# Moving the softmax scale into the copies of q and k, and the row maximum into a plain reduce

## The chip, the cores and the metric

The kernel runs on one core of one Trainium2 chip. Its time is what the device takes for one execution, in microseconds (us). Three runs of the kernel before gave 871.57, 875.91 and 878.39 us, so its median is 875.91 us. One more execution was profiled; it took 872.72 us, and the rows of the profile belong to that one. The engines are called PE (TensorE; its weight loads have a row of their own, PEld), DVE (VectorE), ACT (ScalarE), POOL (GpSimd) and SP (SyncE, which here only issues DMAs).

## The reference

Attention that looks only inside a cluster, and then a feed-forward network with a maximum of three products (B = 4, H = 8, S = 768, D = 64, 16 clusters; 3072 tokens of 512, hidden width 768):

```python
scale = 1.0 / np.sqrt(D)
mask = q_assign[:, :, :, None] == k_assign[:, :, None, :]
scores = scale * np.matmul(q, k.transpose(0, 1, 3, 2))
scores = np.where(mask, scores, -1000000000.0)
scores = scores - np.max(scores, axis=-1, keepdims=True)
attn = np.exp(scores)
attn = attn / (np.sum(attn, axis=-1, keepdims=True) + 1e-09)
out = np.matmul(attn, v)
...
h = np.maximum(np.maximum(x @ w1, x @ w2), x @ w3)
return (h @ w_out).astype(np.float32)
```

`q_assign` and `k_assign` are the cluster whose normalised centroid has the largest product with the row. Since D is 64, the scale is 0.125.

## The kernel before

**Steps.** The attention is cut into 192 steps: 4 batches, 8 heads, 6 blocks of 128 query rows. One step is one call of `scores` (L472): it fills a score tile of 128 x 768 fp32 in PSUM, takes the maximum of each row, the exponential, and the factor 1/sum, splits the result into two fp16 parts and hands them to a DMA that transposes them. Three steps make a group, and `av` (L501) multiplies a group's transposed weights by v. When both heads of a pair are done, `x_split` (L518) makes the input of the FFN.

**Operands.** For a pair of heads the tile `qk` has four planes, AQ, BQ, BK and AK, of 128 rows. A load brings q (64 rows, D of them) and k (64 more) of one head as `stage`; L362 rounds it to fp32r into BQ, and L365 puts the rest that the rounding left into AQ. `qk_moves` (L367) then arranges them: two ACT copies put k's high part into the upper halves of AK (L371) and BK (L372), a DMA brings k's low part to the lower half of AK (L373), and POOL copies q's high part to the lower half of AQ (L374). For the first pair `first_k_moves` (L377) and `first_q_moves` (L385) do this without the DMA, with L381 to L383 on ACT and L388 on POOL. The lower rows of BQ and BK get 16 rows of cluster marks, so that the matrix product itself subtracts a huge number where the clusters differ.

**One step.** Four matmuls (L477, L479) fill the score tile; `big` has three such PSUM buffers, shared with the cluster scores (L405, L406, L413). Then L482 on DVE reads the tile, writes it back multiplied by -1/sqrt(D), and gives through its accumulator the minimum of each row, `nm`, which is the negated maximum of the scaled scores. In the profile it is a pair, TENSOR_SCALAR_CACHE_REDUCE and DVE_READ_ACCUMULATOR. L485 on ACT takes exp(-1 * tile + nm) into SBUF with the row sums `r`; with it the PSUM buffer is free. L486 and L487 on DVE make the factor of each row. In 147 steps ACT applies it and rounds to fp16 (L495) and DVE makes the low part (L496); in 45 steps (`by_pool`) POOL does the multiplication and the low part (L491, L493) and ACT the rounding (L492). L497 on SP issues the transposing DMA from `hl` (four buffers) to `pt` (two).

**Order.** Beside the steps run the preparation of the weights, of v and of the next pair, and the FFN of the group or batch before (`hidden`, L548 to L567, and `outp`, L582 to L593). A table of due steps (`plan`) and priorities (`at_prio`) say when each may come; the last batch's FFN comes after all steps. The order on each engine's queue is then made by the program's scheduler out of these priorities and of modelled durations (`schedule_with_timeline_sim=True`, L761). Each queue runs in its order.

Of the kernel before, what the change touches and what calls it, by code (L numbers as in the profile page):

```python
# [8 lines left out]
F32 = mybir.dt.float32  # L9
# [5 lines left out]
AF = mybir.ActivationFunctionType  # L15
ALU = mybir.AluOpType
AX = mybir.AxisListType
# [6 lines left out]
def kernel(  # L24
# [23 lines left out]
    nc = tc.nc  # L48
    B, H, D, S = qk.shape
    D = D // 2  # L50
# [20 lines left out]
    def big():  # L71
        return ps_big.tile([P, 2 * 512], F32, tag="big", name="big")
# [46 lines left out]
    last = {}  # L119
# [223 lines left out]


    AQ, BQ, BK, AK = range(4)
    HALF = ((0, 512), (512, S))
    qkt = {}
    masks = {}

    def load(b, h):  # L350
        x = stage()
        nc.sync.dma_start(out=x, in_=qk[b, h])
        return x
# [3 lines left out]
    def qk_prep(b, pr, i, pool, again=False):  # L357
# [6 lines left out]
        eng = nc.vector if (b, pr) < (1, 1) and QK_LO[b * NPAIR + pr + (b == 0 and again) * (NPAIR + 1)] else nc.gpsimd  # L364
        last["lo"] = eng.tensor_tensor(t[:, AQ, i], x, t[:, BQ, i].bitcast(F32), op=ALU.subtract)  # L365

    def qk_moves(b, pr):  # L367
        t = qkt[b, pr]
        x = t.bitcast(F32)
        up, dn = slice(0, D), slice(D, 2 * D)  # L370
        nc.scalar.copy(t[up, AK], x[dn, BQ])  # L371
        nc.scalar.copy(t[up, BK], x[dn, BQ])  # L372
        nc.sync.dma_start(out=t[dn, AK].bitcast(F32), in_=x[dn, AQ])  # L373
        nc.gpsimd.tensor_scalar(t[dn, AQ], x[up, BQ], 1.0, 1.0, op0=ALU.mult, op1=ALU.mult)  # L374


    def first_k_moves(xs):  # L377
        t = qkt[0, 0]
        up, dn = slice(0, D), slice(D, 2 * D)
        for i in range(2):  # L380
            nc.scalar.copy(t[up, BK, i], xs[i][dn])  # L381
            nc.scalar.copy(t[up, AK, i], xs[i][dn])
            nc.scalar.copy(t[dn, AK, i], t[dn, AQ, i].bitcast(F32))  # L383

    def first_q_moves():  # L385
        t = qkt[0, 0]
        for i in range(2):
            nc.gpsimd.tensor_scalar(t[D : 2 * D, AQ, i], t[0:D, BQ, i].bitcast(F32), 1.0, 1.0, op0=ALU.mult, op1=ALU.mult)  # L388

    def qk_masks(b, pr):  # L390
        t = qkt[b, pr].bitcast(F32)
# [7 lines left out]
    def cluster_scores(b, pr):  # L399
        t = cl[b, pr] = big()  # L400
        x = qkt[b, pr]
        for lo, hi in HALF:
            for i in range(2):
# [4 lines left out]
    def cluster_early(b, pr):  # L408
        t = cl[b, pr] = big()
        xs = [load(b, 2 * pr + i) for i in range(2)]  # L410
        for lo, hi in HALF:
            for i in range(2):
# [44 lines left out]
    def prep_units(b, pr, pool, again=False):  # L457
        u = [lambda i=i: qk_prep(b, pr, i, pool, again) for i in range(2)]
        if again:
            f = [qk_moves, qk_masks, v_prep]  # L460
        else:
            f = [cluster_scores, qk_moves, cluster_rows] + [v_prep] * (b > 0)
        u += [lambda g=g: g(b, pr) for g in f]
        return u


    K2 = D + C
    SCALE = 1.0 / D**0.5

    def scores(b, h, qt, pt, g, by_pool):  # L472
        aq, bq, bk, ak = (qkt[b, h // 2][:, j, h & 1] for j in range(4))
        t = big()
        qs = slice(qt * P, (qt + 1) * P)
        for lo, hi in HALF:
            nc.tensor.matmul(t[:, lo:hi], aq[:, qs], ak[:, lo:hi], start=True, stop=False)  # L477
        for lo, hi in HALF:
            last["pe"] = nc.tensor.matmul(t[:, lo:hi], bq[0:K2, qs], bk[0:K2, lo:hi], start=False, stop=True)  # L479
        nm = sb.tile([P, 1], F32, tag="nm", name="nm", bufs=6)  # L480
        e = t[:, 0:S]
        last["nm"] = nc.vector.tensor_scalar(e, e, -SCALE, 3.0e38, op0=ALU.mult, op1=ALU.min, accum_out=nm)  # L482
        r = sb.tile([P, 1], F32, tag="r", name="r", bufs=6)
        x = sb.tile([P, S], F32, tag="e", name="e", bufs=3)
        nc.scalar.activation(x, e, AF.Exp, bias=nm, scale=-1.0, accum_out=r)  # L485
        nc.vector.tensor_scalar(r, r, 1.0e-9, 2.0**-14, op0=ALU.add, op1=ALU.mult)  # L486
        nc.vector.reciprocal(r, r)  # L487
        pace[:] = [r[0:1]]
        hl = sb.tile([P, 2, S], F16, tag="hl", name="hl", bufs=4)
        if by_pool:  # L490
            nc.gpsimd.tensor_scalar(x, x, r, 1.0, op0=ALU.mult, op1=ALU.mult)  # L491
            nc.scalar.copy(hl[:, 0, :], x)  # L492
            nc.gpsimd.tensor_tensor(hl[:, 1, :], x, hl[:, 0, :], op=ALU.subtract)  # L493
        else:
            nc.scalar.activation(hl[:, 0, :], x, AF.Copy, scale=r)  # L495
            nc.vector.scalar_tensor_tensor(hl[:, 1, :], x, r, hl[:, 0, :], op0=ALU.mult, op1=ALU.subtract)  # L496
        last["dma"] = nc.sync.dma_start_transpose(out=pt[:, g], in_=hl.rearrange("p a s -> p (a s)"))  # L497
# [159 lines left out]
    with tc.issue_after(last["cw_hi"].ins), tc.issue_after(last["cw_lo"].ins):  # L657
        first[1]()
    cluster_scores(0, 0)
    behind("hi", first_k_moves, xin)  # L660
    first_q_moves()
    behind("lo", vm[0])
    cluster_rows(0, 0)
# [28 lines left out]
    for b in range(B):  # L692
# [3 lines left out]
        if b:  # L696
            visits += [(b, pr, tuple(range(NG))) for pr in range(NPAIR)]
            for pr in range(NPAIR):
                if (b, pr) > (1, 0):
                    t = at + pr * 2 * V  # L700
# [10 lines left out]
    for b, pr, gis in visits:  # L711
        for gi in gis:
            x = (
                sb.tile([P, NB], F32, tag="xs", name="xs", bufs=1),
                sb.tile([P, NB], F32, tag="xt", name="xt", bufs=1),
            )
            for h in (2 * pr, 2 * pr + 1):
                pt = sb.tile([P, G, 2 * QT, P], F16, tag="pt", name="pt", bufs=2)
                for g in range(G):
                    at_prio(step, scores, b, h, gi * G + g, pt, g, by_pool(step))  # L720
                    run_step()
                    step += 1
                units = [lambda a=(b, h, gi, pt, *x): behind("pe", av, *a)]
                if h & 1:
                    units.append(lambda a=(b, pr, gi, *x): x_split(*a))
                plan.setdefault(step + AV_LAG - 1, []).extend((step + AV_LATE, u) for u in units)
# [38 lines left out]
```

## Time and profile before

| what | value |
|---|---|
| median of three runs | 875.91 us |
| the profiled execution | 872.72 us |
| its span from the first to the last instruction | 870.7 us |
| mean granted PE clock, share of full speed | 0.918 |
| L485, the exponential, on ACT | 192 of 898 ns |
| L496, the low part, on DVE | 147 of 1297 ns |
| transposing DMAs (L497) | 192, landing 4.2 us after the issue |
| bytes moved by DMA | 130.99 MB |

A row of the profile names the line, the engine, the operation, the tiles written and read, the shapes and the count; then the busy time in us and the mean length of one instruction in ns; then for how long the engine stood idle ahead of these instructions, and whom it waited for. A row of a stretch gives, for each engine, its busy time and in brackets how many instructions began there. A row in order of time gives start and duration in us.

### The profile page before, as it was taken

The page shows a single profiled execution, that of the slowest core. Times are in us where ns is not written, and L with a number is a line of the kernel's source. Part 1 is how long each engine was busy: PE and PEld are TensorE (multiplying, and loading weights), DVE is VectorE, ACT ScalarE, POOL GpSimd, SP SyncE. Part 2 cuts the span into 40 slices and gives each one's busy share as a digit, 9 for nine tenths or more (in the row PEclk, how much of TensorE's full clock was granted, in tenths as well). Part 3 has the DMA queues.
Part 4 walks back from the last instruction along what each step waited for, and adds up shares of the span by engine and source line. Part 5 has one row for each costly group of instructions (what it writes and reads, how often), then busy time and mean ns, then how long its engine had stood idle before and what let it go on. Part 6 is the DMA issues. An engine that isn't in the chain of part 4 may idle for free. (4 is left out here: it accounts for less than half of the span.)

```text
span 870.7 us, 12115 instructions
## 1 busy us (share of the span) xinstructions
PE 719.7 (83%) x3836; PEld 421.6 (48%) x3836; DVE 613.3 (70%) x1327; ACT 562.4 (65%) x939; POOL 522.9 (60%) x502
## 2 busy tenths in 40 slices
PE   3533766867868989897898999899998999999997
PEld 2312334434544546454555565555554555556463
DVE  7968888799999759885978776876777666411020
ACT  7655677967967577969595967784968467520101
POOL 4696785677963657685867465685684536412111
PEclk9756586869988999998999999999999999999999
DMA  7873988989978499889797978695778586810000
GB/s 248 220 176 72 198 147 195 235 218 244 194 155 191 123 170 182 176 153 216 136 201 129 204 154 154 125 214 117 148 137 137 118 141 114 152 48 1 37 1 36
DMA packets 327679, 130.99 MB, mean 150 GB/s; under 512 B 304192, under 2 KB 313408, under 8 KB 327616
## 3 DMA queue, kind: packets, MB, share of 16 engines
q1 hardware_dynamic: 327616, 130.22, 72.7%
q8 instruction: 30, 0.49, 0.2%
q14 instruction: 33, 0.27, 0.1%
HBM read 38.57 MB, written 7.08 MB: 52 GB/s over the span
## 5 line engine op out<-in xcount | busy, mean ns | idle before, releaser
L485 ACT ACTIVATE e<-big,nm 128x768 f32<-128x768 f32 x192 | 172.2, 898 | 93.9 <-DVE big L482 39.1
L548 PE MATMUL one<-x,w16a 128*128 128x384 f16 x1152 | 205.6, 332 | 18.4 <-DVE p_w L106 3.7
L496 DVE SCALAR_TENSOR_TENSOR hl<-e,r,hl 128x768 f16<-128x768 f32 x147 | 189.4, 1297 | 34.7 <-ACT hl L495 32.4
L482 DVE TENSOR_SCALAR_CACHE_REDUCE big<-big 128x768 f32<-128x768 f32 x192 | 182.1, 960 | 20.2 <-PE big L479 19.4
L477 PE MATMUL big<-qk 128*128 128x512 f32 (+1 forms) x384 | 127.8, 417 | 61.6 <-ACT e L485 56.8
L495 ACT ACTIVATE hl<-e,r 128x768 f16<-128x768 f32 x147 | 134.9, 930 | 42.0 <-DMA pt<-hl 25.1
L548 PEld LDWEIGHTS <-w16a 128*128 128x128 f16 x1152 | 110.6, 99 | 101.1 <-issue 34.2
L479 PE MATMUL big<-qk 80*128 80x512 f32 (+1 forms) x384 | 108.6, 366 | 8.6 <-DMA qk<-cl_t 4.5
L477 PEld LDWEIGHTS big<-qk 128*128 128x128 f32 x384 | 68.0, 209 | 98.1 <-ACT e L485 72.7
L548 PE MATMUL one<-x,w16b 128*128 128x384 f16 x576 | 104.6, 338 | 5.0 <-ACT xt L516 4.4
L507 PE MATMUL one<-pt,v 128*128 128x384 f16 x384 | 82.2, 351 | 29.7 <-POOL v L339 8.0
L493 POOL TENSOR_TENSOR hl<-e,hl 128x768 f16<-128x768 f32 x45 | 77.6, 1728 | 22.4 <-ACT hl L492 22.1
L548 PEld LDWEIGHTS <-w16b 128*128 128x128 f16 x576 | 56.6, 101 | 47.9 <-issue 15.8
L365 POOL TENSOR_TENSOR qk<-stage,qk 128x768 fp32r<-128x768 f32 x32 | 63.8, 2010 | 23.8 <-ACT qk L362 23.5
L479 PEld LDWEIGHTS big<-qk 80*128 80x128 f32 x384 | 65.4, 207 | 21.8 <-DMA qk<-cl_t 5.0
L491 POOL TENSOR_SCALAR e<-e,r 128x768 f32<-128x768 f32 x45 | 47.8, 1064 | 37.0 <-DVE r L487 26.5
L507 PEld LDWEIGHTS <-v 128*128 128x128 f16 x384 | 36.7, 104 | 61.6 <-issue 33.2
L520 POOL TENSOR_TENSOR xs<-xs,xt 128x384 f32<-128x384 f32 x32 | 34.1, 1065 | 51.9 <-ACT xt L516 51.9
L560 DVE SCALAR_TENSOR_TENSOR vf_h<-one,vf_h 128x384 f32<-128x384 f32 x48 | 26.4, 550 | 47.9 <-PE one L548 47.6
L560 DVE SCALAR_TENSOR_TENSOR wf_h<-one,wf_h 128x384 f32<-128x384 f32 x48 | 26.5, 552 | 46.8 <-PE one L548 43.2
L486 DVE TENSOR_SCALAR r<-r 128x1 f32<-128x1 f32 x192 | 27.0, 145 | 45.8 <-ACT e L485 44.9
L492 ACT CAST hl<-e 128x768 f16<-128x768 f32 x45 | 37.3, 829 | 29.3 <-DMA pt<-hl 18.1
(133 smaller groups left out, 1108.2 us busy)
## 6 DMA issues: line engine op xcount, KB each, us to landing
stage<-in_qk_dram SPq DMA_DIRECT2D x36, 384.0 KB, 4.2
stage<-in_v_dram SPq DMA_DIRECT2D x25, 384.0 KB, 3.8
wd<-in_moe_w_dram SPq DMA_DIRECT2D x18, 512.0 KB, 5.1
qk<-qk SPq DMA_DIRECT2D x16, 384.0 KB, 4.4
out_dram<-o SPq DMA_DIRECT2D x24, 256.0 KB, 2.1
pt<-hl SPq DMA_TRANSPOSE x192, 4.2
wd<-in_moe_w_out_dram SPq DMA_DIRECT2D x6, 512.0 KB, 4.4
qk<-cl_t SPq DMA_DIRECT2D x56, 48.0 KB, 2.1
```

Of the source, the lines that this page charges most:

```text
L365: last["lo"] = eng.tensor_tensor(t[:, AQ, i], x, t[:, BQ, i].bitcast(F32), op=ALU.subtract)
L477: nc.tensor.matmul(t[:, lo:hi], aq[:, qs], ak[:, lo:hi], start=True, stop=False)
L479: last["pe"] = nc.tensor.matmul(t[:, lo:hi], bq[0:K2, qs], bk[0:K2, lo:hi], start=False, stop=True)
L482: last["nm"] = nc.vector.tensor_scalar(e, e, -SCALE, 3.0e38, op0=ALU.mult, op1=ALU.min, accum_out=nm)
L485: nc.scalar.activation(x, e, AF.Exp, bias=nm, scale=-1.0, accum_out=r)
L491: nc.gpsimd.tensor_scalar(x, x, r, 1.0, op0=ALU.mult, op1=ALU.mult)
L493: nc.gpsimd.tensor_tensor(hl[:, 1, :], x, hl[:, 0, :], op=ALU.subtract)
L495: nc.scalar.activation(hl[:, 0, :], x, AF.Copy, scale=r)
L496: nc.vector.scalar_tensor_tensor(hl[:, 1, :], x, r, hl[:, 0, :], op0=ALU.mult, op1=ALU.subtract)
L507: nc.tensor.matmul(t[:, 0:NB], vt, pt[:, :, kt, :], start=(kt == 0), stop=False)
L548: nc.tensor.matmul(t[:, 0:NB], w16[jt // JA][:, jt % JA, wa, i, ct], x16[b, gi, ct][:, xa, :], start=(n == 0), stop=(n == 3 * CT - 1),)
L560: nc.vector.scalar_tensor_tensor(m, t[:, 0:NB], 2.0**-24, ms[jt], op0=ALU.mult, op1=ALU.max)
```

## The change

The factor 1/sqrt(D) is put into the copies of k's high part (AK and BK, upper half) and of q's high part (AQ, lower half); the parts left unscaled meet a scaled one in each product, so every product carries the factor once. The ACT copies become activations with a constant factor; POOL's keep their operation with another constant. The DMA of k's low part moves the same bytes between the same places, with its two sides written with the same type. The row maximum becomes a `tensor_reduce` with a negated result that writes nothing back to PSUM, and the exponential reads the scores with scale 1.

```diff
+    SCALE = 1.0 / D**0.5
...
-        nc.scalar.copy(t[up, AK], x[dn, BQ])
-        nc.scalar.copy(t[up, BK], x[dn, BQ])
-        nc.sync.dma_start(out=t[dn, AK].bitcast(F32), in_=x[dn, AQ])
-        nc.gpsimd.tensor_scalar(t[dn, AQ], x[up, BQ], 1.0, 1.0, op0=ALU.mult, op1=ALU.mult)
+        nc.scalar.activation(t[up, AK], x[dn, BQ], AF.Copy, scale=SCALE)
+        nc.scalar.activation(t[up, BK], x[dn, BQ], AF.Copy, scale=SCALE)
+        nc.sync.dma_start(out=x[dn, AK], in_=x[dn, AQ])
+        nc.gpsimd.tensor_scalar(t[dn, AQ], x[up, BQ], SCALE, 1.0, op0=ALU.mult, op1=ALU.mult)
...
-            nc.scalar.copy(t[up, BK, i], xs[i][dn])
-            nc.scalar.copy(t[up, AK, i], xs[i][dn])
+            nc.scalar.activation(t[up, BK, i], xs[i][dn], AF.Copy, scale=SCALE)
+            nc.scalar.activation(t[up, AK, i], xs[i][dn], AF.Copy, scale=SCALE)
...
-            nc.gpsimd.tensor_scalar(t[D : 2 * D, AQ, i], t[0:D, BQ, i].bitcast(F32), 1.0, 1.0, op0=ALU.mult, op1=ALU.mult)
+            nc.gpsimd.tensor_scalar(t[D : 2 * D, AQ, i], t[0:D, BQ, i].bitcast(F32), SCALE, 1.0, op0=ALU.mult, op1=ALU.mult)
...
-    SCALE = 1.0 / D**0.5
...
-        last["nm"] = nc.vector.tensor_scalar(e, e, -SCALE, 3.0e38, op0=ALU.mult, op1=ALU.min, accum_out=nm)
+        last["nm"] = nc.vector.tensor_reduce(nm, e, axis=AX.X, op=ALU.max, negate=True)
...
-        nc.scalar.activation(x, e, AF.Exp, bias=nm, scale=-1.0, accum_out=r)
+        nc.scalar.activation(x, e, AF.Exp, bias=nm, scale=1.0, accum_out=r)
```

## The prediction

> **What bounds the kernel now.** First the page's busy times, then the busy time of each engine in four stretches (columns: stretch, its length, then busy us and count for PE, its weight loads, DVE, ACT and POOL, the granted PE clock, DMA share, GB/s):
>
> ```profile
> PE 719.7 (83%) x3836; PEld 421.6 (48%) x3836; DVE 613.3 (70%) x1327; ACT 562.4 (65%) x939; POOL 522.9 (60%) x502
> ```
> ```profile
> 100.00:250.00 150.00, 109.77 (x515) 63.94 (x514) 131.43 (x300) 119.99 (x201) 114.39 (x109) 0.82 0.94 203
> 250.00:500.00 250.00, 219.09 (x1191) 128.76 (x1189) 202.84 (x453) 185.46 (x310) 160.15 (x138) 0.95 0.86 170
> 500.00:750.00 250.00, 232.52 (x1339) 139.39 (x1338) 182.08 (x403) 176.33 (x300) 153.95 (x138) 0.99 0.77 142
> 750.00:870.00 120.00, 114.61 (x654) 62.64 (x653) 17.31 (x31) 18.39 (x33) 23.35 (x32) 1.00 0.15 38
> ```
>
> The average share of 70% for DVE hides three different stages. From 100 to 250 us DVE is busy 131.43 of 150 us (88%) and the DMA engines 94%: this is where DVE could be the bound. From 250 on PE takes over: 88%, then 232.52 of 250 (93%). From 750 on only TensorE works, on the last FFN. Whatever DVE gains, it cannot touch these last 120 us, and between 500 and 750 it can win at most the 17.5 us in which PE is idle.
>
> Next, who waits for whom (total, times, longest), and the chain of waits that ended last, which this trace follows back to 494 us only:
>
> ```profile
> PE big L477 <- ACT e L485: 56.8, 35, 5.0
> DVE r L486 <- ACT e L485: 44.9, 36, 7.4
> ACT e L485 <- DVE big L482: 39.1, 15, 8.4
> ```
> ```profile
> by line: PE one L548 10.1%; DMA pt<-hl 5.8%; PE one L582 5.4%; issue 2.8%; ACT e L485 2.3%; ACT hl L495 2.2%; DVE big L482 1.5%; DVE hl L496 1.1%; POOL hl L493 1.1%; PE one L507 0.8%; POOL e L491 0.6%; ACT qk L362 0.5%; ACT xt L516 0.5%; PE
> ...
> 494.00 0.83 ACT hl L495
> ```
>
> No engine is alone to blame: TensorE waits for the exponential to free a score buffer, the exponential waits for the row maximum in only 15 of 192 cases, and DVE itself waits for ACT. L482, the line that changes, is on the chain for 1.5% of 870.7, or 13.1 us, out of 870.7 - 494 = 377 us followed.
>
> **DVE: the row maximum.** These groups price the old pair and the new instruction:
>
> ```profile
> L482 DVE TENSOR_SCALAR_CACHE_REDUCE big<-big 128x768 f32<-128x768 f32 x192 | 182.1, 960 | 20.2 <-PE big L479 19.4
> L482 DVE DVE_READ_ACCUMULATOR big<-big 128x1 f32 x192 | 26.5, 138 | 0.1
> L422 DVE STREAM_TRANSPOSE cl_t<-big 128x768 f32<-128x768 f32 x16 | 15.6, 975 | 11.3 <-DMA qk<-cl_t 8.0 <-PE big L413 2.5 <-PE big L406 0.8
> L440 DVE STREAM_TRANSPOSE cl_t<-onehot 128x768 f32<-128x768 f32 x16 | 15.6, 974 | 0.3
> L293 DVE TENSOR_REDUCE vmax<-stage 128x1 f32<-128x768 f32 x12 | 11.3, 945 | 6.8 <-DMA stage<-in_v_dram 6.8
> L222 DVE TENSOR_REDUCE wmx<-wf 128x1 f32<-128x1536 f32 x6 | 10.5, 1746 | 0.1
> L106 DVE TENSOR_REDUCE p_w<-one 128x1 f32<-128x128 f32 x6 | 1.7, 282 | 0.0
> ```
>
> The reduce exists at this width, but from SBUF: 945 ns. Its slope is (1746 - 945)/768 = 1.043 ns per element, so its fixed part is 945 - 801 = 144 ns, and 128 elements from SBUF would take 277; L106 reads 128 from PSUM and takes 282. PSUM thus costs 5 ns, and the transposes say the same (975 from PSUM, 974 from SBUF). I take 950 ns, between 945 and 960. Negation is not in the trace; L293 and L222 take absolute values, L106 none, and all lie on one line, so a change of sign should be free too.
>
> [...]
>
> The tempting sum is now 960 + 138 - 950 = 148 ns, times 192 = 28.4 us. It is wrong if the accumulator read runs under the next instruction, so look at a bunch of them in order of time on DVE and on ACT (start, duration):
>
> ```profile
> 508.09 0.55 DVE L429 TENSOR_REDUCE cl_m<-cl_t 128x24 f32<-128x384 f32 x1 [2.83 <-POOL cl_t L428]
> 508.56 0.96 DVE L482 TENSOR_SCALAR_CACHE_REDUCE big<-big 128x768 f32<-128x768 f32 x1
> 509.43 0.14 DVE L482 DVE_READ_ACCUMULATOR big<-big 128x1 f32 x1
> 509.43 1.00 DVE L482 TENSOR_SCALAR_CACHE_REDUCE big<-big 128x768 f32<-128x768 f32 x1
> 510.35 0.14 DVE L482 DVE_READ_ACCUMULATOR big<-big 128x1 f32 x1
> 510.35 1.00 DVE L482 TENSOR_SCALAR_CACHE_REDUCE big<-big 128x768 f32<-128x768 f32 x1
> 511.26 0.14 DVE L482 DVE_READ_ACCUMULATOR big<-big 128x1 f32 x1
> 511.26 0.55 DVE L434 SCALAR_TENSOR_TENSOR cl_t<-cl_t,rank 128x384 f32<-128x384 f32 x1
> ```
> ```profile
> 509.67 0.90 ACT L485 ACTIVATE e<-big,nm 128x768 f32<-128x768 f32 x1 [1.79 <-DVE big L482]
> 510.47 0.19 ACT L485 ACTIVATION_READ_ACCUMULATOR e<-big,nm 128x1 f32 x1
> 510.58 0.90 ACT L485 ACTIVATE e<-big,nm 128x768 f32<-128x768 f32 x1
> ```
>
> The instruction behind a read starts at the same stamp as the read (509.43, 510.35, 511.26). L434 behind one takes 0.55, as L429, of the same width and with no read ahead of it, does. Only a second L482 behind a read grows, from 0.96 to 1.00. So a pair costs DVE 0.87 to 0.92 us from start to start. How a reduce hands on:
>
> ```profile
> 34.05 0.95 DVE L293 TENSOR_REDUCE vmax<-stage 128x1 f32<-128x768 f32 x1 [0.68 <-DMA stage<-in_v_dram]
> 34.92 0.96 DVE L482 TENSOR_SCALAR_CACHE_REDUCE big<-big 128x768 f32<-128x768 f32 x1
> ```
>
> After 0.87 us. The saving in DVE throughput is therefore 0 to 0.05 us a step, not 0.148. And where maxima come in bunches, the exponentials behind them come 0.91 apart by their own length (510.58 - 509.67), which covers even the 0.05.
>
> [...]
>
> What is left is delay. The first pair of a bunch ends at 509.43 + 0.14 = 1.01 us after its start and the exponential starts 0.10 us later; a reduce of 0.95 lets it start 0.06 earlier. The cover for most steps is that ACT is still busy or that DVE is behind (only 15 waits above); it counts where L482 is on the chain: 13.1 us at 0.92 a pair is 14 pairs. The steps done meanwhile:
>
> ```profile
> 100.00:250.00 150.00, 38.45 (x78) 0.82 0.94 203
> ...
> 500.00:750.00 250.00, 67.89 (x138) 0.99 0.77 142
> ...
> sum 870.00, DVE 191.13; mean DVE 38.23
> ```
>
> (L482 alone; each step has two instructions, so 69 steps from 500 to 750.) 14 in 69 is one step in five; of 192 that is 39, times 0.06 to 0.07 us = 2.3 to 2.7, and I take 2.6 us off the path.
>
> **ACT and POOL: the copies.** A copy with a scale is an ACTIVATE instead of a CAST. Not seen at 64x1536, so from the nearest rows:
>
> ```profile
> L495 ACT ACTIVATE hl<-e,r 128x768 f16<-128x768 f32 x147 | 134.9, 930 | 42.0 <-DMA pt<-hl 25.1 <-issue 7.2 <-DVE r L487 6.1
> L492 ACT CAST hl<-e 128x768 f16<-128x768 f32 x45 | 37.3, 829 | 29.3 <-DMA pt<-hl 18.1 <-POOL e L491 10.8
> L371 ACT CAST qk<-qk 64x1536 fp32r<-64x1536 f32 x16 | 23.5, 1472 | 0.4
> L558 ACT ACTIVATE vf_h<-one 128x384 f32<-128x384 f32 x24 | 11.7, 486 | 28.7 <-PE one L548 28.2 <-DVE vf_h L560 0.2
> ```
>
> With its factor in a tile ACTIVATE costs 930 - 829 = 101 ns more; with a constant factor (L558, as the new copies have) it takes 486 for 384 elements, where a CAST, at (1472 - 829)/768 = 0.837 ns per element, would take 829 - 321 = 508: 22 less, though from PSUM. 32 copies in L371 and L372 and four at the start make 36, so -0.8 to +3.6 us of ACT time over the run. I take 0, by the constant factor; where one is on the chain, the start of that head pair's scores is late by as much. POOL's copies keep their instruction with another constant, and the DMA between copies moves the same bytes: 0, with the same waits. The exponential keeps form and operands: 0.
>
> **The sum.** 872.7 (the profiled execution, 870.7 of it span) - 2.6 = 870.1. The median of the runs shown, 875.9, lies 3.2 above it; off that median it is 873.3, and I say 873. A measurement of this kernel can tell about 1%, 8.8 us, from no change, so this counts as the same.
>
> **The rivals.**
> *Every step gains its delay.* If maximum, exponential and split form the loop in all 192 steps, 0.07 x 192 = 13.4 us: 862. For it: DVE at 88% in 100 to 250, and the 39.1 us of waits. Against: PE at 93% later, DMA at 94% at just that time.
> [...]
> *The queues come out in a worse order (slower).* The order on each queue is the scheduler's, which works with modelled durations (line 761 asks for it), and the replaced instruction may have another. Place: 100 to 250 us, 39 steps (x78), DMA at 94%, so late transposes cannot be made up. If one more maximum (0.95 us) stands ahead of the split L496 in one of three steps there, 13 x 0.95 = 12.4 us: 888. It decides from 10 steps on (9.5 us). For: three maxima in a row stood ahead of other work at 508.56. Against: most modelled lengths stay, and an order can also turn out better.
> *The copies cost their upper price:* 873.3 + 3.6 = 877, still the same. The change does then what it says and shows nothing.
>
> **How the numbers follow.** My forecast 0.47 and the dear copies 0.06: within 1%, 0.53. Every delay 0.19 and the whole read 0.08: faster, 0.27. Worse order 0.20: slower. The likeliest case's own range is 867 to 884. The range of 8 in 10 reaches from 857, leaving the whole read out (0.08), to 888, where the slower rival begins to be cut in half (0.10).
>
> **What would show it.** Right: L482 is one TENSOR_REDUCE of 945 to 960 ns, 192 of them, no read behind it; DVE's busy time falls by about 9 us only (the 191 us that the pairs cover become 182), not by 28; waiting exponentials start about 0.10 us after the reduce ends; L371 and L372 stay near 1472; PE's idle time per stretch stays. [...]

## The result, and the profile after

| | before | after |
|---|---|---|
| median of 20 runs each, taken in turns | 873.92 us | 869.93 us |
| lowest and highest | 867.88, 878.39 | 860.08, 876.87 |
| ratio, 95% interval | | 0.993 (0.9903 to 0.9958) |
| the profiled execution, and its span | 872.72, 870.7 | 869.84, 867.8 |

That is a small gain, under the 1% that the prediction took for the bound. The ratio compares only runs within 1.5% of the fastest of each kernel, and since one run of the kernel after was very quick (860.08), seven of its twenty fall out; over all twenty the means are 873.61 and 870.13 us, a ratio of 0.996 or 3.5 us, and twelve more runs below give 3.2 us. I go by 3.5 us.

The order of the instructions on the five queues is, apart from the replaced instruction itself, the same in both traces but for two places. On ACT one cast of weights (L206) that stood ahead of an exponential, at 124 us, now stands behind it; on DVE, at 482 us, two small instructions (L486 and L101) stand each ahead of a reciprocal instead of behind it. Before, on ACT and on DVE:

```profile
123.61 1.14 ACT L206 CAST w16a<-wf 128x512 f16<-128x512 f32 x2
124.78 0.90 ACT L485 ACTIVATE e<-big,nm 128x768 f32<-128x768 f32 x1
```
```profile
482.37 0.16 DVE L487 RECIPROCAL r<-r 128x1 f32<-128x1 f32 x1
482.44 0.14 DVE L486 TENSOR_SCALAR r<-r 128x1 f32<-128x1 f32 x1
482.50 0.15 DVE L487 RECIPROCAL r<-r 128x1 f32<-128x1 f32 x1
482.57 0.14 DVE L101 TENSOR_SCALAR sc_m<-sc_m 128x1 int32<-128x1 int32 x1
```

And after:

```profile
118.59 0.62 ACT L206 CAST w16a<-wf 128x512 f16<-128x512 f32 x1
119.23 0.90 ACT L486 ACTIVATE e<-big,nm 128x768 f32<-128x768 f32 x1
120.03 0.19 ACT L486 ACTIVATION_READ_ACCUMULATOR e<-big,nm 128x1 f32 x1
120.12 0.61 ACT L206 CAST w16a<-wf 128x512 f16<-128x512 f32 x1
```
```profile
480.70 0.14 DVE L487 TENSOR_SCALAR r<-r 128x1 f32<-128x1 f32 x1
480.77 0.15 DVE L488 RECIPROCAL r<-r 128x1 f32<-128x1 f32 x1
480.83 0.13 DVE L101 TENSOR_SCALAR sc_m<-sc_m 128x1 int32<-128x1 int32 x1
480.89 0.21 DVE L488 RECIPROCAL r<-r 128x1 f32<-128x1 f32 x2
```

Otherwise the scheduler gives the plain reduce the same place as the pair.

The page's busy times, and the four stretches (columns as before):

```profile
PE 728.8 (84%) x3836; PEld 425.7 (49%) x3836; DVE 606.0 (70%) x1135; ACT 562.0 (65%) x939; POOL 521.5 (60%) x502
```
```profile
100.00:250.00 150.00, 112.27 (x520) 65.18 (x519) 124.97 (x251) 115.74 (x194) 112.09 (x108) 0.80 0.91 197
250.00:500.00 250.00, 221.55 (x1184) 128.61 (x1183) 200.39 (x382) 185.36 (x308) 157.10 (x136) 0.94 0.85 171
500.00:750.00 250.00, 233.47 (x1351) 140.62 (x1349) 180.41 (x337) 178.23 (x303) 154.58 (x138) 0.99 0.77 144
750.00:870.00 120.00, 112.26 (x641) 61.20 (x639) 16.10 (x28) 15.68 (x28) 23.31 (x32) 0.99 0.12 32
```

DVE's count falls by 192, from 1327 to 1135, its busy time by 7.3 us only. The stretches do not tell where: from 100 to 250 us it is 6.5 us less, but in the first 100 us it is 4.5 us more (84.11 against 79.63, the rows below, before and after), as some steps fall into another stretch (39 maxima from 100 to 250 us before, 37 now). TensorE's stretch from 500 to 750 is as full as it was, 233 of 250.

```profile
0.00:100.00 100.00, 43.66 (x142) 26.85 (x143) 79.63 (x146) 62.23 (x99) 71.05 (x86) 0.73 0.72 180
```
```profile
0.00:100.00 100.00, 49.28 (x147) 30.13 (x148) 84.11 (x141) 67.03 (x108) 74.38 (x89) 0.91 0.77 190
```

The changed instructions:

```profile
L483 DVE TENSOR_REDUCE nm<-big 128x1 f32<-128x768 f32 x192 | 179.1, 946 | 25.5 <-PE big L480 24.7
```
```profile
L373 ACT ACTIVATE qk<-qk 64x1536 fp32r<-64x1536 f32 x16 | 23.7, 1484 | 0.4
L374 ACT ACTIVATE qk<-qk 64x1536 fp32r<-64x1536 f32 x16 | 23.4, 1465 | 0.0
```

The reduce from PSUM takes 946 ns, with the negation; 950 was forecast. The copies take 1484 and 1465 ns, much as the plain ones did (1472). Then the bunch of three maxima at the same place of the run, in order of time on DVE and on ACT:

```profile
507.05 0.56 DVE L431 TENSOR_REDUCE cl_m<-cl_t 128x24 f32<-128x384 f32 x1 [2.82 <-POOL cl_t L430]
507.52 2.68 DVE L483 TENSOR_REDUCE nm<-big 128x1 f32<-128x768 f32 x3
510.11 0.55 DVE L436 SCALAR_TENSOR_TENSOR cl_t<-cl_t,rank 128x384 f32<-128x384 f32 x1
```
```profile
508.56 0.90 ACT L486 ACTIVATE e<-big,nm 128x768 f32<-128x768 f32 x1 [1.44 <-DVE nm L483]
509.36 0.19 ACT L486 ACTIVATION_READ_ACCUMULATOR e<-big,nm 128x1 f32 x1
509.45 0.89 ACT L486 ACTIVATE e<-big,nm 128x768 f32<-128x768 f32 x1
510.24 0.20 ACT L486 ACTIVATION_READ_ACCUMULATOR e<-big,nm 128x1 f32 x1
510.33 0.90 ACT L486 ACTIVATE e<-big,nm 128x768 f32<-128x768 f32 x1
```

From the first maximum to the work behind the third it is now 510.11 - 507.52 = 2.59 us, where it was 511.26 - 508.56 = 2.70. The first exponential starts 508.56 - 507.52 = 1.04 us after the first maximum, before 1.11: the 0.07 of the forecast. And the exponentials now follow each other every 0.89 us where they came every 0.91: in the bunch it was DVE that paced them. The prediction had taken the 0.91 for their own length.

```profile
PE big L478 <- ACT e L486: 52.1, 30, 5.4
DVE r L487 <- ACT e L486: 45.2, 36, 7.4
ACT e L486 <- DVE nm L483: 28.7, 14, 4.1
```

The exponential's waits for the maximum fall from 39.1 to 28.7 us in total. Single profiles are no proof of that: the same kernel has 35.3 us of them in its later profile (the changed kernel again, below), and a kernel with the old pair has 29.6 (reads at all three places, below); and two runs of the same kernel are up to 17 us apart (860.08 and 876.87). So the parts were tried one by one. The waits in these two, in this order:

```profile
ACT e L486 <- DVE nm L483: 35.3, 14, 8.2
```
```profile
ACT e L486 <- DVE big L483: 29.6, 15, 4.1
```

### The profile page after: what moved, and what is told of

Read it like the earlier page. It is cut to its first block, busy times and chain, and to the rows that moved or that the text cites. A ratio compares the mean times of both kernels' runs of the same rounds, so it can differ in the third digit from the quotient of the medians.

```text
span 867.8 us, 11919 instructions
## 1 busy us (share of the span) xinstructions
PE 728.8 (84%) x3836; PEld 425.7 (49%) x3836; DVE 606.0 (70%) x1135; ACT 562.0 (65%) x939; POOL 521.5 (60%) x502
## 5 line engine op out<-in xcount | busy, mean ns | idle before, releaser
L486 ACT ACTIVATE e<-big,nm 128x768 f32<-128x768 f32 x192 | 171.8, 896 | 84.8 <-DVE nm L483 28.7
L549 PE MATMUL one<-x,w16a 128*128 128x384 f16 x1152 | 209.3, 337 | 18.1 <-DVE p_w L106 3.8
L497 DVE SCALAR_TENSOR_TENSOR hl<-e,r,hl 128x768 f16<-128x768 f32 x147 | 185.3, 1269 | 33.7 <-ACT hl L496 31.8
L483 DVE TENSOR_REDUCE nm<-big 128x1 f32<-128x768 f32 x192 | 179.1, 946 | 25.5 <-PE big L480 24.7
L478 PE MATMUL big<-qk 128*128 128x512 f32 (+1 forms) x384 | 128.6, 418 | 56.1 <-ACT e L486 52.1
L480 PE MATMUL big<-qk 80*128 80x512 f32 (+1 forms) x384 | 110.9, 373 | 10.8 <-DMA qk<-cl_t 6.8
L508 PE MATMUL one<-pt,v 128*128 128x384 f16 x384 | 85.4, 362 | 27.9 <-DMA pt<-hl 9.3
```

The source lines that it names most:

```text
L483: last["nm"] = nc.vector.tensor_reduce(nm, e, axis=AX.X, op=ALU.max, negate=True)
L486: nc.scalar.activation(x, e, AF.Exp, bias=nm, scale=1.0, accum_out=r)
L508: nc.tensor.matmul(t[:, 0:NB], vt, pt[:, :, kt, :], start=(kt == 0), stop=False)
L549: nc.tensor.matmul(t[:, 0:NB], w16[jt // JA][:, jt % JA, wa, i, ct], x16[b, gi, ct][:, xa, :], start=(n == 0), stop=(n == 3 * CT - 1),)
```

## The experiments

Each was run in five rounds in turns with the kernel before; the ratios are to that kernel, with the 95% interval. All edits are to the kernel after, unless it says otherwise. Where the text says that the order is the same, the five queues have the order of the kernel before (in the two kernels that keep the old pair: the copies alone, and reads at all three places) or that of the kernel after (in the others); the two orders differ only in the two places named above. The diffs leave out lines that allocate a tile; `...` marks lines left out between.

**The copies alone** (same order).

```diff
-  last["nm"] = nc.vector.tensor_reduce(nm, e, axis=AX.X, op=ALU.max, negate=True)
+  last["nm"] = nc.vector.tensor_scalar(e, e, -1.0, 3.0e38, op0=ALU.mult, op1=ALU.min, accum_out=nm)
...
-  nc.scalar.activation(x, e, AF.Exp, bias=nm, scale=1.0, accum_out=r)
+  nc.scalar.activation(x, e, AF.Exp, bias=nm, scale=-1.0, accum_out=r)
```

> The scaled copies as in the changed kernel, the row maximum as the old pair with factor -1 and its accumulator read. Theory (the gain is the shorter maximum ahead of the exponential): no gain, ratio to the kernel before 0.998 to 1.002. Rival (the copies gain): 0.993. Rival (the copies cost, hidden by a larger gain of the maximum): above 1.002.

Measured: 1.0004 (0.9969 to 1.0039). The copies neither gain nor cost.

**The reduce alone** (same order): the reduce and the exponential's scale put into the kernel before.

```diff
-  last["nm"] = nc.vector.tensor_scalar(e, e, -SCALE, 3.0e38, op0=ALU.mult, op1=ALU.min, accum_out=nm)
+  last["nm"] = nc.vector.tensor_reduce(nm, e, axis=AX.X, op=ALU.max, negate=True)
...
-  nc.scalar.activation(x, e, AF.Exp, bias=nm, scale=-1.0, accum_out=r)
+  nc.scalar.activation(x, e, AF.Exp, bias=nm, scale=1.0, accum_out=r)
```

> The plain reduce and the exponential with scale 1, the copies as before; the factor 1/sqrt(D) is left out altogether, so the output is that of a sharper softmax. Theory: the whole gain, ratio about 0.993. Rival (the copies gain): 1.000.

Measured: 0.9967 (0.9931 to 1.0002); the means are 868.7 against 872.6 us. The interval just touches no change, but the size is that of the whole change. **The changed kernel again**, which was run later beside other kernels:

> The changed kernel once more, to tell its gain from that of the maximum alone: 0.996 to the kernel before if the maximum alone makes it (868.7 against 872.6 there), 0.993 if the copies add something.

Measured: 0.9969 (0.9936 to 1.0002), means 868.6 against 871.8. That is the size of the maximum alone, and 0.993 lies just outside the interval. So the gain is the maximum's, and there are two ways in which it could arise: the exponential starts earlier, or DVE has fewer instructions. The next two put an accumulator read back on DVE, but not ahead of the exponential.

**A read behind the split** (same order).

```diff
-  nc.vector.scalar_tensor_tensor(hl[:, 1, :], x, r, hl[:, 0, :], op0=ALU.mult, op1=ALU.subtract)
+  nc.vector.scalar_tensor_tensor(hl[:, 1, :], x, r, hl[:, 0, :], op0=ALU.mult, op1=ALU.subtract, accum_out=ac)
```

> The changed kernel with an accumulator output added to the 147 low-part instructions of the split on DVE: the accumulator reads are back on DVE's queue, but behind the exponential and the split. Theory (what counts is the 0.065 us of delay between scores and exponential): nearly all of the gain stays, ratio to the kernel before 0.993 to 0.996. Rival (what counts is DVE's queue getting shorter, wherever the read stands): three quarters of the gain are gone, 0.998.

Measured: 1.0012 (0.9976 to 1.0048). The gain is gone, against the theory. The reads in order of time on DVE:

```profile
504.25 1.00 DVE L498 SCALAR_TENSOR_TENSOR hl<-e,r,hl 128x768 f16<-128x768 f32 x1
505.18 0.08 DVE L498 DVE_READ_ACCUMULATOR hl<-e,r,hl 128x1 f32 x1
505.18 1.01 DVE L498 SCALAR_TENSOR_TENSOR hl<-e,r,hl 128x768 f16<-128x768 f32 x1
```

Again the next instruction starts at the read's stamp. But this stamp is later than it would be without the read: from the start of a split to the start of the instruction right behind it the median is 0.938 us here and 0.929 in the kernel after (by the start times in the traces, which go down to 1 ns; the 72 splits of usual length, under 1.1 us, with work right behind them). The page of this kernel has DVE as little busy as that of the kernel after (607.0 against 606.0 us):

```profile
PE 723.1 (83%) x3836; PEld 423.6 (48%) x3836; DVE 607.0 (69%) x1282; ACT 561.3 (64%) x939; POOL 518.7 (59%) x502
```

**A read behind the row factor** (same order).

```diff
-  nc.vector.tensor_scalar(r, r, 1.0e-9, 2.0**-14, op0=ALU.add, op1=ALU.mult)
+  nc.vector.tensor_scalar(r, r, 2.0**-14, 1.0e-30, op0=ALU.mult, op1=ALU.max, accum_out=ac)
```

> The changed kernel with an accumulator output added to the first of the two small instructions that make the row factor, 192 reads between the exponential and the split. The value is the same (the 1e-9 is below the rounding of a sum that is at least 1, and a maximum with 1e-30 stands in its place). Theory (only the delay ahead of the exponential counts): 0.993 to 0.996. Rival (any delay of 0.07 to 0.14 us in the loop from maximum to split counts alike): the gain is gone, 0.999 to 1.005.

Measured: 1.0014 (0.9978 to 1.0049). Gone as well, though the bunch of maxima is the quick one there:

```profile
507.68 2.67 DVE L483 TENSOR_REDUCE nm<-big 128x1 f32<-128x768 f32 x3
510.27 0.55 DVE L436 SCALAR_TENSOR_TENSOR cl_t<-cl_t,rank 128x384 f32<-128x384 f32 x1
510.74 0.14 DVE L488 TENSOR_SCALAR_CACHE_REDUCE r<-r 128x1 f32<-128x1 f32 x1
510.81 0.08 DVE L488 DVE_READ_ACCUMULATOR r<-r 128x1 f32 x1
510.81 0.15 DVE L488 TENSOR_SCALAR_CACHE_REDUCE r<-r 128x1 f32<-128x1 f32 x1
```

**Both placed reads together, and reads at all three places** (same order): the two edits above in one kernel, and these with the pair of the first experiment.

> The changed kernel with reads at the two placed spots together, behind the first small instruction of the row factor (192) and behind the split (147), 339 in all, and none behind the maximum. If every read costs 0.013 to 0.018 us wherever it stands (the slopes of the kernels with 0, 192 and 531 reads): 868.6 + 4.4 to 6.1 = 873 to 875, ratio 1.001 to 1.003. If one read in the loop costs the gain and further ones nothing: 1.000. If the read ahead of the exponential is what counts and the two single runs were chance: 0.996.

> The scaled copies, with accumulator reads at three places of every step: behind the maximum (the old pair), behind the first small instruction of the row factor (192) and behind the split (147). Theory that every read on DVE costs about 0.02 us of the run's time wherever it stands (3.5 us for 192): 873.6 + 3.5 + 2.8, ratio 1.007. Rival (the reads lie in the shadow of the next instruction, and only the one ahead of the exponential counts): 1.000. Rival (the two placed reads took the gain away by chance of the runs): 1.000 as well, and then the first two kernels with one read each belong to 0.996.

Measured: 1.0009 (0.9973 to 1.0046) with 339 reads, which does not decide between the expectations, and 1.0040 (1.0010 to 1.0070) with 531, which leaves out the 1.000 of the two rivals and lies below the theory's 1.007. In one table, by the means of all runs against the kernel before in the same call:

| reads on DVE, and where | mean, us against before |
|---|---|
| none (reduce alone; changed again) | -3.9; -3.2 |
| 147 behind the split | +0.5 |
| 192 (copies alone: behind the maximum; behind the factor) | +0.2; +0.1 |
| 339 | +1.2 |
| 531 | +3.6 |

From none to 531 it is 7.1 us, or 13 ns a read; from none to 192 3.7 us, or 19 ns; from none to 147 4.0 us, or 27 ns. Each step alone is about as large as its interval; the row of them is not. A read counts, and where it stands makes no difference that these runs can see. Nor can they tell an equal price for every read from a higher one for the first in each step, since 147, 192 and 339 reads lie within 1.1 us of each other. That the two orders differ in two places does not explain the loss: the kernels with a placed read have the order of the kernel after. That the old instruction also wrote its result back to PSUM makes none either: behind the factor there are 192 reads without such a write, in the copies alone 192 with it.

The traces show part of the price. Taken as behind the split, from start to start with work right behind, the median is 0.865 us for the maximum without a read (kernel after) and 0.875 with one (kernel before), in 164 places each; for the first small instruction of the row factor, where something other than the reciprocal follows, it is 0.061 us without (kernel after) and 0.071 with a read (read behind the row factor), in 79 places each. The kernel before, which has no read behind the split or the row factor either, has 0.932 and 0.065 us there. So a read puts the next instruction off by 10 ns behind the maximum and by 6 to 10 ns behind the other two. For 192 reads behind the maximum that is 1.9 us, half of what was measured, if all of it came through to the end of the run; no run shows that it does.

**The maximum over 512 columns, over 640, and over 512 read twice** (another order each; three kernels, the new lines of each one after the other).

```diff
-  last["nm"] = nc.vector.tensor_reduce(nm, e, axis=AX.X, op=ALU.max, negate=True)
...
+  last["nm"] = nc.vector.tensor_reduce(nm, e[:, 0:512], axis=AX.X, op=ALU.max, negate=True)
...
+  last["nm"] = nc.vector.tensor_reduce(nm, e[:, 0:640], axis=AX.X, op=ALU.max, negate=True)
...
+  e2 = t[:, 0:512].rearrange("p (a d) -> p a d", a=1).broadcast_to([P, 2, 512])
+  last["nm"] = nc.vector.tensor_reduce(nm, e2, axis=AX.XY, op=ALU.max, negate=True)
```

> The changed kernel with the maximum taken over the first 512 of 768 columns only (the exponential is over all 768): 256 x 1.043 = 267 ns less on DVE and ahead of the exponential in each step. The scheduler gives another order. One step in five on the path: 39 x 0.267 = 10 us, 860. All steps on the path: 51 us, 819. PE and DMA bound the rest: under 3 us, 867 or more.

> The changed kernel with the maximum over the first 640 columns: 128 x 1.043 = 133 ns less in each step, 25.6 us of DVE in all, another order again. If DVE's time matters by one step in five: 868.6 - 5 = 864. If it does not: as the changed kernel, 868.6, and what differs from that is the price of an order, within 4 us either way.

> The changed kernel with the maximum over the first 512 columns read twice, 1024 elements: the values of the narrow one, at 267 ns more than the changed kernel and 534 ns more than the narrow one in each step. Another order. If DVE's time counts fully: 868.6 + 51 = 920. If one step in five is on the path: 879. If DVE's time does not matter, as the narrow one has it: 870 to 873.

Measured: 0.9994 (0.9962 to 1.0026) for 512, 1.0046 (1.0015 to 1.0077) for 640, 1.0117 (1.0079 to 1.0156) for 1024. Each fence is of one kernel: the split and the maximum over 512, the split in the kernel after, the maximum over 640 and the one over 1024:

```profile
L497 DVE SCALAR_TENSOR_TENSOR hl<-e,r,hl 128x768 f16<-128x768 f32 x147 | 199.2, 1361 | 52.9 <-ACT hl L496 52.6
L483 DVE TENSOR_REDUCE nm<-big 128x1 f32<-128x512 f32 x192 | 128.9, 680 | 24.7 <-PE big L480 23.5
```
```profile
L497 DVE SCALAR_TENSOR_TENSOR hl<-e,r,hl 128x768 f16<-128x768 f32 x147 | 185.3, 1269 | 33.7 <-ACT hl L496 31.8 <-issue 1.0 <-POOL qk L366 0.5
```
```profile
L483 DVE TENSOR_REDUCE nm<-big 128x1 f32<-128x640 f32 x192 | 153.3, 814 | 24.0 <-PE big L480 22.8
```
```profile
L484 DVE TENSOR_REDUCE nm<-big 128x1 f32<-128x1024 f32 x192 | 230.5, 1211 | 14.2 <-PE big L480 13.3
```

The narrow maximum takes 680 ns, 50 us less of DVE in the run, and the run is no shorter than that of the kernel after. DVE waits 52.6 us for ACT's part of the split instead of 31.8, and the split itself takes 199 us instead of 185 (33.7 and 190.5 us in the later profile of the kernel after). The 640 columns are slower than all 768, with less work, and miss both of their expectations: what is left to differ is the order, so I put some 7 us down to it (875.5 against 868.6), though no run has the same work in two orders. The wide one takes 51 us more and costs 881.4 - 868.6 = 12.8 us: one part in four, near the one in five that the chain gave, but with 7 us either way for its own order anything from 6 to 20 us. The narrow one should have gained 10 us by one in five and is 1.4 us slower than the kernel after (870.0 against 868.6): 7 us for its order would leave some 4 us of that gain missing. So in these runs longer maxima are paid for and shorter ones not in full, if at all.

**One small instruction more, and one fewer** (another order each).

```diff
-  last["nm"] = nc.vector.tensor_reduce(nm, e, axis=AX.X, op=ALU.max, negate=True)
+  nc.vector.tensor_reduce(mx, e, axis=AX.X, op=ALU.max)
+  last["nm"] = nc.vector.tensor_scalar_mul(nm, mx, -1.0)
```

> The changed kernel with the negation as an instruction of its own on 128x1 behind the maximum, 192 of about 0.15 us, 0.19 us more between maximum and exponential. The scheduler gives another order. One step in five on the path: 39 x 0.19 = 7 us more than the changed kernel, 877. All steps: 36 us more, 906. Hidden: 870.

```diff
-  nc.vector.tensor_scalar(r, r, 1.0e-9, 2.0**-14, op0=ALU.add, op1=ALU.mult)
   nc.vector.reciprocal(r, r)
...
-  nc.scalar.activation(xs[mn, :], t[mn, 0:NB], AF.Copy, scale=2.0**-14)
-  nc.scalar.activation(xt[mn, :], t[ot, 0:NB], AF.Copy, scale=2.0**-14)
+  nc.scalar.activation(xs[mn, :], t[mn, 0:NB], AF.Copy, scale=1.0)
+  nc.scalar.activation(xt[mn, :], t[ot, 0:NB], AF.Copy, scale=1.0)
```

> The changed kernel without the first small instruction of the row factor (L487): the reciprocal is taken of the sum itself, and the factor 2**14 that it carried is left out there and in the two copies behind the attention product. 192 DVE instructions of 0.14 us fewer between exponential and split, the opposite of the negation apart (which cost 5.8 us more than the changed kernel). The scheduler gives another order. If small links in the loop cost alike: 868.6 - 5.8 = 863, ratio to the kernel before 0.990. If the loop is bound elsewhere and the negation's loss was its order: 0.995 to 1.000.

Measured: 1.0038 (1.0007 to 1.0068) with the negation apart, and 0.9960 (0.9936 to 0.9984) without the small instruction. The first comes close to one step in five (874.4 against 877 expected). The second was meant to beat both kernels and does not beat the kernel after: means 868.3 against 868.6. DVE's time goes into waits there too:

```profile
L496 DVE SCALAR_TENSOR_TENSOR hl<-e,r,hl 128x768 f16<-128x768 f32 x147 | 200.9, 1372 | 45.5 <-ACT hl L495 44.0 <-DMA qk<-cl_t 0.7 <-issue 0.5
```
```profile
PE big L478 <- ACT e L486: 73.5, 38, 6.2
```

Against the profile of the kernel after the split grew by 16 us, its wait for ACT by 12, and TensorE waits 73.5 us for a score buffer instead of 52.1 (against its later profile by 10 and 10 us, and instead of 57.5). Both kernels have another order, so neither price is free of it.

## Why the prediction was right, and where it was not

**The size and the side.** The sum said 2.6 us less; the runs say 3.5, and "within 1%". That holds; that 2.6 comes so near to 3.5 is luck, as the step on delay below shows.

**The reduce from PSUM** was taken at 950 ns and measures 946; from SBUF it is 945 in L293 before and 944 there after.

**The copies** were taken at 0, with 3.6 us as the far end. They measure 1484 and 1465 ns against 1472 for the plain ones, and alone they give 1.0004.

**The tempting 28.4 us.** The step that looked at the order of time and threw this sum out was the one that mattered: the page's 138 ns of each read are not DVE's time. DVE's busy time fell by 7.3 us, where 9 were forecast and 28 would have been the sum of rows; the time that the maxima cover fell from 191 us to 179, where 182 were forecast. The chance of 0.08 for the whole read stands for this sum in full. No run shows a read that goes whole: where work follows at once, it starts at the read's own stamp (505.18 and 510.81 us above), and the runs put the price of a read at 13 to 27 ns.

**"What is left is delay": this step failed.** The prediction put the read's cost in DVE's queue at next to nothing, because exponentials 0.91 apart would cover it, and priced only the 0.06 to 0.07 us by which the exponential starts earlier. The delay is there (1.04 us against 1.11), but it is not shown to be what gains: no run delays the exponential without a read in the same order. Reads placed where they do not delay the exponential at all take the whole gain away, and from none to 531 reads costs twice as much as from none to 192. What counts is the read, at any of the three places, at 13 to 27 ns each; for 192 reads that is 2.5 us or more, which by luck is the size that was forecast for another reason. Part of it can be seen: the 6 to 10 ns by which a read puts off the next start, and in the bunch the exponentials that came every 0.91 us and now come every 0.89. The prediction looked only at whether the next instruction shares the read's stamp, and missed that the stamp itself is later; its one comparison, L434 with L429, is of two different operations. How the rest arises stays open, and so does why so small a delay reaches the end of the run when 267 ns less in each maximum gained nothing.

**The share on the path.** One step in five, from the chain, was near for added work: the wide maximum says one in four, the negation one in six (5.8 of 36 us), each give or take the price of its order. It was not good for work taken away: 50 us less of DVE gained nothing beside the changed kernel, where it should have gained 10, more than the 7 us put down to an order. The prediction's reason, PE at 93% and DMA at 94% in their stretches, fits this, but no run took those bounds away, so it is argued and not shown.

**The slower rival.** Its condition did not come about: but for two places the order stayed as it was. Its price was of the right kind, if the 7 us of the 640 columns are their order's: 12 were forecast.

## What to carry to other kernels

Before a row's time is counted as a saving, look in the order of time whether the next instruction starts with it or after it, and then compare start to start with and without it over many places; accumulator reads of 79 to 138 ns were worth 13 to 27 ns each here, over three places, and 6 to 10 of them show so. A share of the chain came near for work that was added; work taken away gained less than it here, and longer waits elsewhere stood in its place. And where a scheduler orders the queues by modelled durations, ask first whether the order changes: replacements that leave it almost as it was can be compared, others bring, as far as these runs show, several us of order with them.

## What the runs showed of the hardware

A maximum over 512, 640, 768 and 1024 elements of PSUM took 680, 814, 946 and 1211 ns, so 1.04 ns per element and about 148 ns beside; the 1211 are 512 columns read twice, and the access pattern paid for both readings. A read behind a maximum took 138 ns, behind the split or the row factor 79 to 81 ns, and in all three places work that followed at once started at the same stamp as the read (509.43, 505.18 and 510.81 us). That start came later than where there is no read: 0.875 against 0.865 us behind a maximum, 0.938 against 0.929 to 0.932 behind the split, 0.071 against 0.061 to 0.065 behind the row factor.
